# Linear attention and a gated convolution layer in one kernel: from four tokens a partition with 64-token tails to nine tokens a partition

## The chip, the cores and the metric

The kernel runs as one program on one core of a Trainium2 chip. Its engines are TensorE (PE: matmuls, with weight loads shown apart as PEld), VectorE (DVE), ScalarE (ACT), GpSimd (POOL) and SyncE (SP, which here only issues transfers). The metric is the device time of one execution in microseconds, smaller is better. Three executions of the kernel before gave 233.52, 234.02 and 235.5 us: the median is 234.02 us.

## The reference

Eight batches, eight heads, 576 tokens of 64 channels. First a linear attention, then a layer that multiplies a causal five-tap gate with a projection:

```python
def phi(x):
    proj = np.einsum('bhsd,df->bhsf', x, w_phi)              # 64 -> 128 features
    proj = proj - np.max(np.abs(proj), axis=-1, keepdims=True)
    return np.concatenate([np.exp(proj), np.exp(-proj)], axis=-1)
q_p, k_p = (phi(q), phi(k))
kv = np.einsum('bhsf,bhsd->bhfd', k_p, v)
z = np.sum(k_p, axis=2)
num = np.einsum('bhsf,bhfd->bhsd', q_p, kv)
den = np.einsum('bhsf,bhf->bhs', q_p, z)[..., None] + 1e-06
x = num / den                                                # then (8, 576, 8*64)
...
for k in range(K):                                           # K = 5 taps, causal
    gate_pre += conv_w[k][None, None, :] * xp[:, k:k + S, :]
gate = 1.0 / (1.0 + np.exp(-gate_pre))
val = x @ w_val                                              # 512 x 512
return (gate * val @ w_out).astype(np.float32)
```

Inputs and output are fp32; the matmuls take bf16 operands.

## The kernel before

**Tiling.** A batch's 576 tokens are split into a main part of 512 and a tail of 64. In the main part partition p holds the tokens 4p to 4p+3 of a head (four "planes" of 128 tokens). A unit is one pair of heads of one batch: 2 heads x 4 planes x 128 rows, 1024 tokens of two heads, in 32 main units; four tail units hold the tails of two batches and all eight heads each, again 1024 rows. So there are 36 units with the same work.

**Steps of a unit.** The names are those of the functions `op_...`; the lines are those of the profile.
- T (L331): eight 128x128 transposes of k and q into one PSUM bank; Tc (L224 on DVE, L222 on ACT) copies the 1024 columns to SBUF.
- PK and PQA (`tokproj`, L342): k and q times w_phi with tokens on the partitions, eight matmuls each, 64 rows deep, alternating between the two halves of the rows and between two PSUM banks. mKa, mK, mQa, mQ (L356) take the largest magnitude of each row, one bank (512 columns) at a time.
- K0 to K3 (L388): ACT takes exp of plus and minus the projected k, a bank each. The row maximum of k is not put in there: E (L382) makes exp of minus and plus the maximum, and V (L408, POOL) multiplies v by it and adds the column that gives z.
- PQ (L466): q's projection with features on the partitions; SH (L476): eight matmuls that subtract q's row maximum; Qa and Q (L484): four exps of a bank each.
- KV (L445, L450): per unit four sums (two signs, two heads) of four planes and a tail, 20 matmuls of full 128 rows with 65 columns; the tail rows of the other batch are kept at zero in VZ. KVM (L224, L222) copies them out.
- NUM (L509, tails L523): 16 matmuls of 65 columns; XN (L534, L536) divides by the last column; XP (L545, L548) brings channels back to the partitions by a DMA transpose from SP's queue into XT (main) or XH (tails).

**The layer.** GA (L604) makes the gate by matmuls with diagonal weights, 64x64 tiles, 32 matmuls for half of a batch's channels in two PSUM banks, with the shifts of planes split into up to two pieces a tap. TH (L612) is ACT's tanh over two banks, VAa and VAb (L617) the projection by w_val, GV (L633) gate times value on DVE, OUT (L642) the projection by w_out, OE (L649 on ACT, L651 on DVE) the halving on the way out of PSUM, ST (L663) the store. GAt, THt, GVt, OUTt, OEt, STt (L673, L681, L690, L695, L704, L716) do the same for the tails of two batches.

**Order.** All of it is one list written out by hand, `ORDER`: each word is a step, with its PSUM banks after @ and its engine after a colon. Every engine takes its instructions strictly in that order and waits for the operands and the banks that a step needs. The loads (L299, L304) are issued by POOL and turn fp32 to bf16 on the way; POOL's queue thus holds loads and the V steps in one order.

Of the kernel before, what the change touches and what calls it, by code (L numbers as in the profile page):

```python
# [20 lines left out]
SM = 512  # L21
ST = S - SM
E1 = D + 1
PL = 144
TL = 80
NG = B // 2
NU = 9 * NG

# [4 lines left out]
LD7 LD6 CK0 CQ0 T1@1 LD2 ND0:A W20 Tc1:D PK1@2,5 mKa1 PQA1@6,1 K01 mK1 mQa1 mQ1 T0@0 LD0 Tc0:A  # L33
PQ1@3,4 PK0@7,6 K11 K21 mKa0 T2@0 E1 Tc2:D K31 K00 SH1 Qa1 LD1 PK2@1,0 mK0 mKa2 LD3 mK2 PQA2@3,5
mQa2 ZV0:P LD8 K20 mQ2 T3@2 E0 Tc3:D PQA0@3,5 mQa0 mQ0 K02 K10 K30 E2 K22 PK3@7,6 mKa3 PQA3@2,5
LD4 mQa3 Q1 LD9 PQ2@3,4 SH2 LD10 mK3 K32 K12 T4@0 Tc4:D PK4@1,0 K03 Qa2 mQ3 V0:P K23 V1:P KV1@3 Q2
LD5 V2:P mKa4 K33 K04 KVM1:D NUM1@4 PQ3@6,3 SH3 mK4 XN1 LD11 K13 KV2@2 K24 LD31 PQA4@7,4 KVM2:D E3
mQa4 K14 mQ4 PQ0@1,5 K34 SH0 LD30 Qa3 Qa0 NUM2@6 PQ4@2,0 T5@4 T6@1 Q3 SH4 Q0 XN2 Qa4 E4 Tc5:D
Tc6:D PK5@7,6 mKa5 K05 PQA5@3,1 PK6@2,5 mQa5 Q4 LD13 K15 mK5 LD12 V3:P K25 KV3@3 mQ5 V4:P mKa6 K06
LC0 K35 KVM3:D E5 V5:P LD32 LD39 PQ5@0,1 TP0@7 mK6 Vb0:P NUM3@3 CW0 XP1 XN3 K16 XP2 T7@7 Tc7:D K26  # L40
SH5 Qa5 PQA6@6,2 mQa6 PK7@3,7 mKa7 KV4@4 PQA7@6,0 mQ6 mQa7 XP3 K36 T8@5 Tc8:D mK7 PQ6@2,6 Q5
KVM4:A SH6 K07 NUM4@4 mQ7 XN4 E6 PK8@0,1 K17 mKa8 Qa6 K27 T9@2 Tc9:D Q6 XP4 PQA8@3,5 V6:P PQ7@4,6
SH7 mQa8 LD15 mK8 K08 K37 PQA9@2,3 mQ8 mQa9 KV5@7 KVM5:D mQ9 T10@5 Tc10:D K18 PQ8@0,2 SH8 Qa7
PK9@4,7 mKa9 T11@3 E7 V7:P Q7 PK10@5,6 Tc11:D K28 mKa10 LD14 DG0:P Qa8 K38 KV6@3 Q8 K09 NUM5@0 mK9
KVM6:D NUM6@2 XN5 K010 mK10 KV7@0 K29 K110 XN6 K19 KVM7:D T12@5 PK11@1,4 mKa11 K210 HL0:P Tc12:D
XP6 LD16 K39 GA0@2 K310 mK11 K011 NUM7@6 VAa1@0 LD40 XN7 E8 VAb1 TH0 GV1 V8:P PK12@2,5 PQA10@3,6
K111 PQ9@1,7 SH9 VAa2@0 K211 mQa10 mKa12 LD19 VAa0@3 mK12 E9 LD17 K311 Qa9 VAb0 mQ10 KV8@4 KVM8:D
VAb2 GV0 PQA11@1,6 K012 V9:P Q9 mQa11 K212 PQ10@4,7 SH10 mQ11 K112 T13@3 Tc13:D NUM8@1 XN8 E10
K312 Qa10 Q10 GA1@5 TH1 PK13@3,4 mKa13 NUM0@1 V10:P KV10@7 XN0 KVM10:D XP5 XP0 XP8 E11 E12 K013
mK13 VAa3@5 GV2 PQ11@6,1 SH11 K113 Qa11 V11:P VAb3 GV3 LD18 K213 NUM10@2 XN10 T14@0 Tc14:D Q11  # L50
KV11@7 XP7 PQA12@5,6 K313 GA2@2 E13 TH2 PK14@0,1 mQa12 mQ12 PQA14@4,5 OUT1@6 OE1:A KVM11:D
PQA13@7,2 mQa14 V12:P V13:P mKa14 LD34 K014 mQ14 mQa13 K114 PQ12@3,4 SH12 XP10 KV12@6 mQ13 T15@5
Qa12 KVM12:A Tc15:D OUT2@7 Q12 mK14 K214 NUM11@2 E14 PQ13@0,6 SH13 Qa13 XN11 XP11 NUM12@4 OE2:D
XN12 T16@2 VAa6@3 PK15@7,0 mKa15 GA3@4 mK15 K314 V14:P VAa4@1 Q13 Tc16:D VAb4 K015 TH3 PQA15@6,2
GV4 K215 K315 PQ14@5,4 SH14 mQa15 K115 mQ15 VAa5@1 VAb5 PK16@0,6 Qa14 VAb6 Q14 KV13@7 GV5 mKa16
mK16 Vb9:P K016 VAa7@2 T17@1 GV6 E15 V15:P Tc17:D LD33 KVM13:A KV14@5 LD22 HL1:P NUM13@3 K116 K216
PQ15@0,7 KVM14:A VAb7 XN13 K316 SH15 GV7 PK17@1,3 mKa17 Qa15 K017 Q15 K117 LD35 mK17 XP13
# [42 lines left out]
OUT30@1 OEt3:A ST27 ST25 ST29 OE31:A ST28 STt3 ST31 OE30:D ST30  # L100
"""


class _U:
    pass

@with_exitstack
def kernel(  # L110
    ctx: ExitStack,
    tc: tile.TileContext,
# [30 lines left out]


    units = []
    for G in range(NG):
        for kind in range(9):
            u = _U()
            u.G = G
# [614 lines left out]
```

## Time and profile before

| what | before |
|---|---|
| three executions | 233.52, 234.02, 235.5 us |
| span of the profiled execution, first to last instruction | 232.5 us |
| mean granted TensorE clock in it | 0.972 |
| busy PE / DVE / ACT / POOL | 205.8 / 184.2 / 188.6 / 125.4 us |
| instructions PE / DVE / ACT / POOL | 3497 / 335 / 419 / 142 |
| DMA packets, bytes | 62002, 30.90 MB |
| queue of POOL's converting loads: packets, share of 16 engines | 36144, 58.2% |

The profile gives no time of its own for the profiled execution; its span of 232.5 us lies 1.5 us below the median of the three times, which hold the start and the end around the span as well. A busy time counts a matmul or a vector instruction from its start to its end, and neighbours on one engine overlap at their ends, so what an instruction costs its queue is the distance from its start to the next one's start, a little less than its duration.

### The profile page before, as it was taken

The numbers are of one execution on the slowest core, as the hardware profiler recorded it, in microseconds if no ns is written. First come the engines' busy times: TensorE is split into PE (matmuls) and PEld (weight loads), VectorE is DVE, ScalarE is ACT, GpSimd is POOL, SyncE is SP. The second block draws the span as 40 slices with busy tenths as digits, with TensorE's granted clock in tenths as the row PEclk, the third lists the DMA queues.
The fourth block names the chain that finished last, engine by engine and source line by source line (L and its number), as shares of the span: only waits on it lengthen the run. The fifth ranks groups of instructions, "written<-read, shape, count | busy, mean of one in ns | idle before, by whom it ended". The sixth has DMA issues, their size and how long they took to land.

```text
span 232.5 us, 8372 instructions
## 1 busy us (share of the span) xinstructions
PE 205.8 (89%) x3497; PEld 139.5 (60%) x3516; DVE 184.2 (79%) x335; ACT 188.6 (81%) x419; POOL 125.4 (54%) x142
## 2 busy tenths in 40 slices
PE   1286797888999989899999999999899999999991
PEld 1264675666666746567666766766476667564550
DVE  5559669999989979699999879897799788554451
ACT  3189869999997988599999979998899999934251
POOL 8909935999979437774919751564526241100000
PEclk9998579999999999999999999999999999999997
DMA  8997995979999942999994992499903928126195
GB/s 151 246 198 97 106 180 80 92 101 178 129 194 128 139 32 32 129 257 177 128 114 68 180 186 92 39 115 126 214 6 37 169 77 259 38 52 200 27 355 185
DMA packets 62002, 30.90 MB, mean 133 GB/s; under 512 B 33420, under 2 KB 59148, under 8 KB 61964
## 3 DMA queue, kind: packets, MB, share of 16 engines
q0 software_dynamic: 36144, 14.29, 58.2%
q1 hardware_dynamic: 25468, 15.78, 33.6%
q8 instruction: 27, 0.44, 0.8%
q10 hardware_dynamic: 352, 0.30, 0.4%
q14 instruction: 11, 0.09, 0.2%
HBM read 30.48 MB, written 9.44 MB: 172 GB/s over the span
## 4 chain that ended last, share of the span: by engine, by line
PE 69%; ACT 11%; DMA 9%; DVE 5%; issue 3%; SPq 1%; POOL 1%; POOLq 0%; DVEq 0%; ACTq 0%
PE PS L617 11%; PE PS L642 10%; PE PS L342 7%; PE PS L604 7%; PE PS L476 7%; PE PS L445 6%; PE PS L331 6%; DMA XT<-XN 6%; PE PS L509 5%; ACT QTIL L484 5%; ACT KTIL L388 3%; DMA kT<-in_k_dram 3%; PE PS L466 3%; PE PS L681 2%; DVE MQ L356 2%
## 5 line engine op out<-in xcount | busy, mean ns | idle before, releaser
L408 POOL TENSOR_TENSOR VT<-vN,E 128x1024 bf16<-128x1024 bf16 x27 | 51.5, 1907 | 60.4 <-issue 34.2
L388 ACT ACTIVATE KTIL<-PS 128x512 bf16<-128x512 f32 x128 | 76.7, 666 | 5.3 <-DVE MK L356 5.1
L484 ACT ACTIVATE QTIL<-PS 128x512 bf16<-128x512 f32 x128 | 71.0, 666 | 2.5 <-PE PS L476 1.1
L356 DVE TENSOR_REDUCE MK<-PS 128x4 f32<-128x512 f32 x72 | 47.9, 683 | 7.5 <-PE PS L342 7.2
L356 DVE TENSOR_REDUCE MQ<-PS 128x4 bf16<-128x512 f32 x72 | 47.4, 683 | 1.3 <-PE PS L342 1.2
L342 PE MATMUL PS<-W,T 64*128 64x128 bf16 x576 | 29.6, 227 | 5.8 <-DVE T L224 1.9
L617 PE MATMUL PS<-XT,WVAL 128*128 128x512 bf16 x128 | 33.8, 380 | 0.3 <-DMA XT<-XN 0.3
L342 PEld LDWEIGHTS <-T 64*128 64x128 bf16 x576 | 18.3, 98 | 21.8 <-issue 11.9
L642 PE MATMUL PS<-WOUT,GV 128*128 128x512 bf16 x111 | 29.9, 380 | 1.2 <-issue 0.5
L633 DVE SCALAR_TENSOR_TENSOR GV<-GATE,PS 128x512 bf16<-128x512 bf16 x32 | 21.6, 681 | 5.9 <-ACT GATE L612 3.1
L445 PE MATMUL PS<-VT,KTIL 128*128 128x65 bf16 x512 | 25.4, 198 | 0.8 <-DVE T L224 0.6
L536 DVE TENSOR_TENSOR XN<-PS,RCP 128x512 bf16<-128x512 f32 x36 | 24.9, 691 | 1.2
L445 PEld LDWEIGHTS <-KTIL 128*128 128x128 bf16 x512 | 22.8, 100 | 3.7 <-DVE T L224 0.8
L476 PE MATMUL PS<-nident,MQ 128*128 128x128 bf16 x288 | 23.9, 229 | 0.5 <-issue 0.5
L612 ACT ACTIVATE GATE<-PS 128x1024 bf16<-128x1024 f32 x16 | 16.7, 1044 | 8.8 <-PE PS L604 8.7
L476 PEld LDWEIGHTS <-MQ 128*128 128x128 bf16 x288 | 17.6, 102 | 9.5 <-issue 8.8
L224 DVE COPY T<-PS 128x1024 bf16<-128x1024 bf16 x31 | 21.1, 684 | 2.7 <-PE PS L331 2.3
L509 PEld LDWEIGHTS <-QTIL 128*128 128x128 bf16 x512 | 19.3, 99 | 5.5 <-DVE KVS L224 1.1
L509 PE MATMUL PS<-KVS,QTIL 128*128 128x65 bf16 x512 | 21.4, 196 | 1.3 <-DVE KVS L224 0.8
L450 PE MATMUL PS<-VZ,KTt 128*128 128x65 bf16 x128 | 21.9, 196 | 0.0
L604 PE MATMUL PS<-XT,DIAG 64*64 64x384 bf16 (+3 forms) x512 | 20.6, 299 | 1.0 <-issue 0.8
L642 PEld LDWEIGHTS <-GV 128*128 128x128 bf16 x128 | 11.3, 98 | 12.4 <-issue 0.6
(73 smaller groups left out, 304.1 us busy)
## 6 DMA issues: line engine op xcount, KB each, us to landing
out_dram<-OS SPq DMA_DIRECT2D x14, 512.0 KB, 3.8
kN<-in_k_dram POOLq DMA_DIRECT2D x7, 512.0 KB, 9.0
qN<-in_q_dram POOLq DMA_DIRECT2D x7, 512.0 KB, 8.4
vN<-in_v_dram POOLq DMA_DIRECT2D x7, 512.0 KB, 6.9
vF<-in_v_dram SPq DMA_DIRECT2D x2, 512.0 KB, 7.6
out_dram<-OSt SPq DMA_DIRECT2D x8, 128.0 KB, 2.4
out_dram<-OS SPq DMA_DIRECT2D x4, 256.0 KB, 2.9
qT<-in_q_dram POOLq DMA_DIRECT2D x8, 64.0 KB, 5.2
```

What stands on the lines that cost most here:

```text
L342: nc.tensor.matmul(PS[:, bank[rg], blk * P:(blk + 1) * P], u.T[r, i, blk, :], W2[r, :], start=True, stop=True,)
L356: nc.vector.tensor_reduce(dst, PS[:, bank, :].rearrange("p (b f) -> p b f", f=F), AX.X, ALU.max, apply_absolute_value=True,)
L388: nc.scalar.activation(u.KT[:, ft, rg, :, :].rearrange("p b f -> p (b f)"), PS[:, u.PK[rg], :], AF.Exp, scale=1.0 if ft == 0 else -1.0,)
L408: eng.tensor_tensor(dst[:, :, :, 0:D], x.unsqueeze(1).to_broadcast([n, 2, 8, D]), e.unsqueeze(3).to_broadcast([n, 2, 8, D]), ALU.mult,)
L445: nc.tensor.matmul(o, u.KT[:, ft, rg, h2 * 2 + j2, :], u.VT[:, ft, (h2 * 2 + j2) * 2 + rg, :], start=(c == 0), stop=False,)
L476: nc.tensor.matmul(PS[:, u.PQ[rg], blk * P:(blk + 1) * P], u.MQ[:, rg, blk:blk + 1].to_broadcast([P, P]), nident[:, :], start=False, stop= ...
L484: nc.scalar.activation(u.QT[:, ft, rg, :, :].rearrange("p b t -> p (b t)"), PS[:, u.PQ[rg], :], AF.Exp, scale=1.0 if ft == 0 else -1.0,)
L509: nc.tensor.matmul(ps[:, j2, x * E1:(x + 1) * E1], u.QT[:, ft, rg, h2 * 2 + j2, :], u.KVS[:, (ft * 2 + h2) * E1:(ft * 2 + h2 + 1) * E1], s ...
L536: nc.vector.tensor_tensor(u.XN[:, :, :, :], nv[:, :, :, 0:D], RCP[:, :, :].unsqueeze(3).to_broadcast([P, 2, 4, D]), ALU.mult,)
L604: nc.tensor.matmul(ps[c, par, j0 * P:j1 * P], DIAG[r, dt, 4 - dl, :], mv, start=(i == 0), stop=(i == len(parts) - 1), skip_group_check=True,)
L617: nc.tensor.matmul(PS[:, m.val[jt], :], WVAL[:, dt, jt * P:(jt + 1) * P], XTs[m.b % 2][:, dt, :, 16:PL], start=(dt == 0), stop=(dt == 3),)
L642: nc.tensor.matmul(PS[:, bank[0], :], m.GV[:, jt, j * P:(j + 1) * P], WOUT[:, jt, :], start=(jt == 0), stop=(jt == 3),)
```

## The change

The tokens are laid out anew: partition p of a half holds the nine tokens 9p to 9p+8 of a head, and the two heads of a pair lie in the two halves of the partitions (64 rows each). A main unit is a pair of heads and eight of the nine planes (2 x 8 x 64 = 1024 rows), 32 of them as before; the ninth planes of all heads of a batch make a tail unit of 512 rows, eight of them. One load brings a whole batch of k, q or v, tails included, in pieces of nine tokens; w_val and w_out come as fp32 from SP's queue and are converted by POOL.

- T: sixteen transposes of 64 rows into two banks; C copies them out in one instruction with its halves interleaved. KV: 36 matmuls of 64 rows, the two heads in two banks, no zero rows any more.
- MK, MQ, K0, K1, X0, X1: one instruction over two banks where there were two over one each.
- The gate: GF makes all four channel blocks of a batch in four banks, five taps of sixteen 32x32 tiles, 80 matmuls of 512 columns. A copy HL of the last four planes in front of the first ones, one row lower, gives the shifts whole, so no tap is split. GT, VT, HT, GW do the ninth plane of each batch; OT, OF, SU that of two batches.
- OUT is split into OA and OB of two matmuls each, as VA and VB are. Tail results, and the last batch's main ones, come back to XT by transposes on PE and a copy (XP with a bank, XX) instead of DMA transposes. Small tiles (row maxima, E, reciprocals, KV sums) get a place for every unit instead of rotating buffers, and `read` tells the scheduler that readers of a bank need not wait for readers of its earlier contents on other engines.
- A new `ORDER` with 1076 words for 1116.

Taps no longer go by 32 matmuls for half a batch but by 80 for a whole one; the steps that keep their count are OUT, VA/VB, NUM of the main units, SH of the main units. The core of the diff:

```diff
-        return src[name][b, h0:h1, 0:SM, :].rearrange("h (p j) d -> p h (j d)", j=4)
-
+        return src[name][b, 2 * h0:2 * h1, :, :].rearrange("(hp t) (p j) d -> (t p) hp (j d)", t=2, j=J)
...
+    def read(inst, bank):
+        for x in bank:
+            for other in gone[x]:
+                if other.engine != inst.ins.engine:
+                    tc.declare_no_dep(inst.ins, other, reason="covered by the wait for the matmuls")
+            held[x].append(inst.ins)
...
-                nc.tensor.transpose(u.Tps[:, n, blk, :], col(u, name, blk), ident_bf[:, :])
+                for h2 in range(2):
+                    r = slice(h2 * 64, h2 * 64 + 64)
+                    nc.tensor.transpose(
+                        u.Tps[:, h2, (4 * x + blk) * 64:(4 * x + blk + 1) * 64],
+                        main[name, u.b][r, u.hp, 2 * blk:2 * blk + 2, :].rearrange("p j d -> p (j d)"),
+                        ident_bf[r, r],
+                    )
...
+        copy(
+            eng, u.T[:, :, :, :].rearrange("p i b (h t) -> p h (i b) t", h=2),
+            u.Tps.rearrange("p h (x t) -> p h x t", t=64), u.TB,
+        )
...
-        nc.vector.tensor_reduce(
-            dst, PS[:, bank, :].rearrange("p (b f) -> p b f", f=F),
+        read(nc.vector.tensor_reduce(
+            dst[:, :, 0:n], banks(*bank)[:, :, c0:c0 + n * F].rearrange("p a (b f) -> p a b f", f=F),
...
+    def exps(dst, bank, n, ft):
+        read(nc.scalar.activation(
+            dst, banks(*bank)[:, :, 0:n * P].rearrange("p r (x t) -> p r x t", t=dst.shape[-1]),
...
     def op_KV(i, bank):
         u = units[i]
-        u.KVps = PS[:, bank[0], 0:4 * E1]
-        ut = tail_of[u.G]
+        t = units[32 + u.b]
+        u.KV = bank
         for ft in range(2):
-            for h2 in range(2):
-                o = u.KVps[:, (ft * 2 + h2) * E1:(ft * 2 + h2 + 1) * E1]
-                for c in range(4):
-                    j2, rg = c // 2, c % 2
+            for j in range(J):
+                for h2 in range(2):
+                    r = slice(h2 * 64, h2 * 64 + 64)
+                    if j < 8:
+                        kt, vt = u.KT[r, ft, j % 2, j // 2, :], u.VT[r, ft, j, :]
+                    else:
+                        kt, vt = t.KT[r, ft, u.hp % 2, u.hp // 2, :], t.VT[r, ft, u.hp, :]
                     nc.tensor.matmul(
-                        o, u.KT[:, ft, rg, h2 * 2 + j2, :],
-                        u.VT[:, ft, (h2 * 2 + j2) * 2 + rg, :],
-                        start=(c == 0), stop=False,
+                        PS[:, bank[h2], ft * E1:(ft + 1) * E1], kt, vt, start=(j == 0), stop=(j == 8),
                     )
-                nc.tensor.matmul(
-                    o, ut.KT[:, ft, h2, u.hp, :],
-                    VZ[u.G % 2][u.b % 2][:, ft, 2 * u.hp + h2, :],
-                    start=False, stop=True,
-                )
-
...
+            u.XPps = PS[:, bank[0], 0:128].bitcast(BF16).rearrange("p (a t) -> p a t", a=4)
+            for hp in range(HP):
+                for h2 in range(2):
+                    r = slice(h2 * 64, h2 * 64 + 64)
+                    nc.tensor.transpose(u.XPps[r, hp, :], u.XN[r, hp, :], ident_bf[r, r])
+            return
...
+        t = xt(b)[:, :, :].rearrange("p a (s c) -> p a s c", c=64)
+        copy(eng, t[:, :, 0:4, 1:64], t[:, :, 9:13, 0:63])
...
+    def taps(m, dts):
+        XT = xt(m.b)
+        for tap in range(5):
+            for dt in dts:
+                for r in range(4):
+                    rows, cols = slice(r * 32, r * 32 + 32), slice((r ^ dt) * 32, (r ^ dt) * 32 + 32)
+                    nc.tensor.matmul(
+                        PS[cols, m.gate[dt], :], DIAG[rows, dt, tap, :],
+                        planes(XT, rows, dt, tap),
+                        start=(tap == 0), stop=(tap == 4), skip_group_check=True,
+                    )
...
+    def op_GF(b, bank):
+        m = batches[b]
+        bank = sorted(bank)
+        for x in range(4):
+            m.gate[x] = bank[x]
+        taps(m, range(4))
...
+    def op_GT(b, bank):
+        m = batches[b]
+        m.tb = bank = sorted(bank)
+        XT = xt(b)
+        for s in range(2):
             for tap in range(5):
-                for dt, r, c, par in quarters(q2):
-                    nc.tensor.matmul(
-                        ps[c, par, q2 * P:(q2 + 1) * P], DIAG[r, dt, tap, :],
-                        XH[r, dt, :, 12 + tap:12 + tap + ST],
-                        start=(tap == 0), stop=(tap == 4), skip_group_check=True,
-                    )
+                for r in range(2):
+                    for x in range(2):
+                        dt = 2 * x + s
+                        rows = slice(r * 64, r * 64 + 64)
+                        cols = slice((r ^ x) * 64, (r ^ x) * 64 + 64)
+                        nc.tensor.matmul(
+                            PS[cols, bank[x], s * 64:s * 64 + 64], DIAG2[rows, dt, tap, :],
+                            XT[rows, dt, (8 + tap) * 64:(9 + tap) * 64],
+                            start=(tap == 0), stop=(tap == 4), skip_group_check=True,
+                        )
...
+    def op_OA(n, bank):
...
+        outmm(m.out[j], lambda jt: m.GV[:, jt, j, :, :].rearrange("p i t -> p (i t)"), (0, 1))
...
+    def outmm(bank, lhs, jts):
+        for jt in jts:
+            nc.tensor.matmul(PS[:, bank, :], lhs(jt), WOUT[:, jt, :], start=(jt == 0), stop=(jt == 3))
...
```

## The prediction

> **What bounds the kernel now.** I read the busy times first, then the busy times by stretch, then the chain that ended last, then single groups in the timeline to get prices. In the page:
>
> ```profile
> PE 205.8 (89%) x3497; PEld 139.5 (60%) x3516; DVE 184.2 (79%) x335; ACT 188.6 (81%) x419; POOL 125.4 (54%) x142
> ...
> PE 69%; ACT 11%; DMA 9%; DVE 5%; issue 3%; SPq 1%; POOL 1%; POOLq 0%; DVEq 0%; ACTq 0%
> ```
>
> Three engines are within 22 us of one another, and 69% of the chain is PE. The table by stretch (length, then busy us of PE, PEld, DVE, ACT, POOL, granted clock, DMA share, GB/s) shows how the bound moves:
>
> ```profile
> 30.00:60.00 30.00, 26.47 (x491) 19.56 (x488) 28.62 (x54) 28.53 (x68) 22.82 (x27) 0.97 1.10 124
> ...
> 180.00:210.00 30.00, 29.79 (x538) 20.04 (x544) 21.57 (x40) 24.20 (x54) 6.19 (x6) 1.00 0.56 126
> ```
>
> Up to 60 us DVE and ACT are full; later PE is. The chain in order of time (start, length, what) dates the change of bound and gives the first prices:
>
> ```profile
> 3.83 7.29 DMA kT<-in_k_dram
> ...
> 56.08 1.22 PE PS L604 x32
> ...
> 118.61 0.63 PE PS L523 x32
> ```
>
> The first taps run at 56.1 us, and from there to the last matmul's end at 227.7 nearly all pieces are PE. At the start 7.3 us go to the first tail load. After the last matmul come 4.8 us: a halving on DVE and the last store.
>
> **Prices.** Of a group that follows another without a gap I take start to start. In PE's timeline (start, length with the last one's drain, what):
>
> ```profile
> 142.03 0.40 PE L342 MATMUL PS<-W,T 64*128 64x128 bf16 x8
> 142.27 0.38 PE L466 MATMUL PS<-T,W 64*128 64x512 bf16 x2
> ...
> 144.26 0.39 PE L331 MATMUL PS<-ident_bf,kT 128*128 128x128 bf16 x4
> ...
> 144.70 0.29 PE L445 MATMUL PS<-VT,KTIL 128*128 128x65 bf16 x4
> ...
> 146.75 0.40 PE L342 MATMUL PS<-W,T 64*128 64x128 bf16 x8
> 147.08 1.04 PE L642 MATMUL PS<-WOUT,GV 128*128 128x512 bf16 x3
> ...
> 148.38 0.77 PE L673 MATMUL PS<-XH,DIAG 64*64 64x128 bf16 x40
> 149.08 1.07 PE L681 MATMUL PS<-XH,WVAL 128*128 128x128 bf16 x16
> 149.99 0.29 PE L445 MATMUL PS<-VT,KTIL 128*128 128x65 bf16 x4
> ...
> 150.62 0.66 PE L509 MATMUL PS<-KVS,QTIL 128*128 128x65 bf16 x16
> 151.11 0.29 PE L445 MATMUL PS<-VT,KTIL 128*128 128x65 bf16 x4
> ...
> 152.39 0.62 PE L476 MATMUL PS<-nident,MQ 128*128 128x128 bf16 x8
> 152.84 0.65 PE L509 MATMUL PS<-KVS,QTIL 128*128 128x65 bf16 x16
> ```
>
> - Projection of eight (L342): 0.24 us, if the next group has the same tile shape; 0.33 if PE changes the shape of its tiles (146.75 to 147.08). So a change of shape costs 0.1.
> - Transposes T: 0.44. SH: 0.45. KV: 20 matmuls 0.63, 31.5 ns each. NUM: 16 in 0.49. Tail taps L673: 40 in 0.70, 0.60 without the change, so 15 ns each although every one has its own weights. Tail value projection: 0.91.
> - Taps of half a batch (L604): 1.22 in the chain, 1.12 without the change. Tail NUM (L523): 32 in 0.63, 0.53 without it, 16.6 ns each. Four matmuls of 512 columns (L617, L642): 0.86. PQ, two of them side by side: 0.22, a quarter of that, though 0.33 pass to the next start.
> - ACT (start, length, what):
>
> ```profile
> 101.01 1.06 ACT L612 ACTIVATE GATE<-PS 128x1024 bf16<-128x1024 f32 x1
> 101.91 0.34 ACT L382 ACTIVATE E<-MK 128x8 f32<-128x8 f32 x2
> ```
>
> so two banks in one instruction take 0.90, where one bank takes 0.485 (pairs of L484 last 1.08 with an end of 0.11). On DVE 512 columns take 0.60 (L356 at 110.17, 110.77, 111.36), 0.53 of which are columns; 1024 in one instruction I take as 1.13, an estimate from these.
>
> **The change, PE.** Sum before: T 36 x 0.44 = 15.8; projections 72 x 0.24 = 17.3; PQ 7.9; SH 16.2; KV 32 x 0.63 = 20.2; NUM 15.7 and tails 2.1; taps 16 x 1.12 = 17.9; values and OUT 64 x 0.86 = 55.0; tail layer 4 x (0.60 + 0.91 + 0.86) = 9.5; together 177.6. In the order of before the tile shape changes 164 times: 16.4. Sum 194.0. From the first taps on it is 165.7, in 171.6 us that passed: PE is 96.5% packed.
>
> After, the new operations have no row of their own. T is 16 matmuls of 64 rows and 64 columns, alternating between the halves of the rows and two banks; KV 36 of 65 columns in the same form. Upper bound: the 29 to 31.5 ns of L342 and of KV now, that is 0.48 and 1.08 us. Lower bound: half a 65-column matmul (31.5 / 2 ns), about the 15 ns of L673. The nearest rows are L673 and L523, small tiles that take turns, at 15 and 16.6 ns; I take 15 to 15.5: T 0.24, KV 0.56. Taps: 80 matmuls with sixteen tiles at once; L604 streams four at once, 32 in 1.12. If sixteen do, 5 x 0.22 = 1.1 us a batch; at 15 ns each 1.2, which I take; if they overlap no better than four, 80 x 35 ns = 2.8.
>
> Sum after: T 32 x 0.24 + tails 8 x 0.23 = 9.5; projections 17.3; PQ 7.9; SH 16.2; KV 32 x 0.56 = 17.9; NUM 15.7 + 8 x 0.27 = 17.9; taps 8 x 1.2 = 9.6; GT 8 x 0.6 = 4.8 (40 matmuls a batch, not for two); VT 8 x 0.48 = 3.8; values, OUT, OT 58.4; transposes for XP 8 x 0.12 + 4 x 0.22 = 1.8; together 165.1. Tile shapes change 226 times in the new order: 22.6. Sum 187.7, 6.3 less than before: taps -8.3, T -6.3, KV -2.3; changes of shape +6.2, tail steps +4.
>
> The Trainium skill (TensorEngine Tiling, Restrictions and Gotchas) says that different row tiles cannot access one PSUM bank at a time; the taps of GF write four row tiles to each bank. In this trace L604 has two row tiles to a bank, and 32 x 512 columns in 1.12 us is four at a time, so the trace does not bear it out; by that rule the 2.8 of above would hold, 240 us, which is counted in (a).
>
> **ACT and DVE.** ACT before: 288 exps x 0.485 + 40 us of the rest = 180. After: 128 x 0.90 + 32 tail exps x 0.49 + the rest = 173. DVE before: row maxima 144 x 0.60 = 86.4, all 177. After: 64 x 1.13 + 16 x 0.60 = 81.9, two more copies (HL of 1008 columns about 0.8, between the 0.60 of T's copy and 1.2; XX), smaller tail steps: 181. So the two-bank steps save 7 us on ACT and DVE gains 4, hidden as long as PE is fuller: a batch has 23.1 to 24.2 us of PE and 22.2 to 22.7 of DVE. That cover is only 1 us a batch. POOL stays at about 123 (V 69 and 9, loads 30 x 0.95, conversion of the two weights about 9, diagonals 5); its V steps are late by nothing in this sum. The waits that `read` and the fixed small tiles take away I put at nothing: in the view of waits PE's largest sum for a vector engine after the start is 4.0 us (L342's weights for T's copy), so at most that would come back. The converting queue has fewer and longer pieces; on the chain its loads count only at the start.
>
> **The path.** Start: in before ACT's steps ahead of the first taps are 41.4 us by these prices, and the taps start at 56.1, so 14.7 us are lost to loads and first dependencies. After, the first GF stands behind only six K pairs, five Q pairs and two tails: ACT 27.0, DVE 26.9, PE 17.0, POOL 32.7. The same loss: 27.0 + 14.7 = 41.7 us, and POOL's 32.7 fit. From there PE has 187.7 - 17.0 = 170.7; packed like before, / 0.965 = 176.9, to 218.6. At the end of before four batches' layers were left to fill PE; now only the last batch's remain, behind XN, a transpose, XX and HL (0.85 + 0.2 + 0.35 + 0.8), about 3 us with little to run: 221.6. Then a halving 0.6 and a store of 128 KB, 2.4 by its row, 0.3 for the issue: 224.9. With the 1.5 us by which before's median exceeds its span, 226.4: I say 227, 3% below 234.02. Its own range is 220 to 233: the start 4 us either way, packing 0.95 to 0.98, KV and T 3 us more.
>
> **Rivals.**
> (a) Small matmuls have a floor: at 29 ns KV is 1.04 and T 0.46, 32 x 0.70 = 22 us more, at 22 ns half of it: 238 to 250. Taps that overlap only four at once (2.8) would add 8 x 1.6 = 13: 240. For it: full-array KV and NUM go at 31 ns now; against it: L673 and L523 at 15 to 17 ns with weights of their own. It turns the result slower from about 19 ns on. The Trainium skill (TensorE: Matmul & The Clock Gate, Wait — 56ns, not 53.3ns?) gives 25 ns as the least distance; by it this rival would hold, near 250, but L673 goes below it here.
> (b) DVE becomes the bound: C now writes with its halves interleaved. If that copy costs a cycle per column like the fp32 steps, 1.13 instead of 0.60, DVE has 4 x 0.53 = 2.1 more a batch, 24.5, and passes PE's 23.7; in the 30 us from 90 on, with every engine in play, DVE was 0.91 busy, and 24.5 / 0.91 is 26.9 us a batch where the forecast has 24.6 (23.7 / 0.965); over seven batches 16: 243, slower. It decides from about 0.83 us a copy. Against it: T's copy takes 0.60 for 1024 now, and its inner runs stay 64 long.
> (c) Banks: GF takes four of eight banks at once, until two tanhs of 0.90 have read them, and T, PK, PA, PQ, KV, N take two each. If PE stands 1.7 us a batch for want of banks, 8 x 1.7 = 14: 240, slower; it decides from 0.9 us. Nothing in before shows it, its gate took two.
> (d) More gain: fewer loads and maxima bring the first GF to 36 us, PE packed 0.98: 36 + 174.2 + 3 + 3.3 + 1.5 = 218.
>
> **How the numbers follow.** The forecast 0.48, (a) 0.15, (b) 0.13, (c) 0.10, (d) 0.14. A measurement of this kernel tells apart about 1%. Faster by more: nearly all of the forecast (0.45), all of (d), and some 0.05 of mild forms of (a) to (c): 0.64. Within 1%: 0.08. Slower: 0.28. The range takes (d) and the middle of (a) to (c): 217 to 242.
>
> **What would show it.** Right: GF in about 1.3 us with 80 matmuls; KV's 36 in 0.56 and T's 16 in 0.24; first GF near 42 us; two-bank exps 0.90 apart, row maxima 1.13; PE between 180 and 200 busy and the chain mostly PE. Wrong: KV near 1 us (a); DVE the first in the chain with copies over 0.83 (b); PE waiting before GF, T or PK for ACT or DVE readers of its banks (c).

## The result and the profile after

The changed kernel took 256.54 us (median of 253.63, 259.45, 257.75 and 255.33), the kernel before in the same runs 234.12. The ratio is 1.086, with a 95% interval of 1.080 to 1.092: 8.6% slower, where 3% faster was forecast. Ratios here and below leave out executions in which the whole core ran disturbed, and each stands against the kernel before on the same chip; medians take in all. The profiled execution is the one of 253.63 us, with a span of 251.8. Its page:

```profile
PE 206.3 (82%) x4730; PEld 134.3 (53%) x4756; DVE 186.8 (74%) x295; ACT 184.1 (73%) x305; POOL 110.2 (44%) x142
...
PE 55%; DVE 15%; DMA 13%; ACT 10%; issue 5%; SPq 1%; ACTq 0%; DVEq 0%
```

PE is busy as long as before (205.8) in a span that is 19 us longer, and PE's part of the chain fell from 69% to 55%. What grew there are DVE, DMA and "issue". The table by stretch (columns as before) tells where:

```profile
30.00:60.00 30.00, 25.04 (x635) 16.90 (x634) 24.39 (x39) 24.42 (x40) 21.57 (x31) 0.94 0.73 102
60.00:90.00 30.00, 21.98 (x531) 13.94 (x529) 19.32 (x32) 19.18 (x31) 10.13 (x12) 0.83 0.79 116
90.00:120.00 30.00, 25.63 (x539) 15.61 (x541) 20.69 (x32) 21.32 (x37) 10.31 (x11) 0.83 0.81 140
...
180.00:210.00 30.00, 26.59 (x642) 17.01 (x646) 25.40 (x39) 24.82 (x46) 11.27 (x13) 1.00 0.27 60
```

Before 60, PE, DVE and ACT are each some 25 of 30 us busy. From 60 to 90 none is above 22, and the granted clock falls to 0.83 in two stretches. The chain in order of time (start, length, what) names what stands there:

```profile
35.45 5.06 DMA XT<-XN
41.73 2.36 PE PS L585 x80
...
65.03 11.24 DMA XT<-XN
78.04 2.29 PE PS L585 x80
...
97.87 8.35 DMA XT<-XN
107.16 1.86 PE PS L585 x39
110.71 1.08 PE PS L585 x30
137.30 1.34 PE PS L585 x80
```

L585 is the taps GF. The first one starts at 41.73; the next ones start 36.2, 29.2, 30.1, 25.9, 27.8, 27.8 and 18.2 us after one another. Ahead of three of them stands a DMA transpose of XN into XT.

The prices themselves are as forecast. PE's timeline (start, length, what), then DVE's:

```profile
152.95 0.43 PE L441 MATMUL PS<-VT,KT 64*128 64x65 bf16 x16
153.22 0.19 PE L441 MATMUL PS<-VTt,KTt 64*128 64x65 bf16 x2
153.25 0.42 PE L441 MATMUL PS<-VT,KT 64*128 64x65 bf16 x16
153.51 0.19 PE L441 MATMUL PS<-VTt,KTt 64*128 64x65 bf16 x2
153.54 0.39 PE L355 MATMUL PS<-W,T 64*128 64x128 bf16 x8
...
154.85 0.29 PE L333 MATMUL PS<-ident_bf,kN 64*128 64x64 bf16 x8
154.97 0.28 PE L333 MATMUL PS<-ident_bf,qN 64*128 64x64 bf16 x8
```

```profile
126.84 1.21 DVE L373 TENSOR_REDUCE MKA<-PS 128x8 f32<-128x1024 f32 x1
127.97 1.21 DVE L373 TENSOR_REDUCE MQA<-PS 128x8 bf16<-128x1024 f32 x1
...
76.69 0.68 DVE L198 COPY T<-PS 128x1024 bf16<-128x1024 bf16 x1
77.29 0.42 DVE L198 CAST KVSA<-PS 128x260 bf16<-128x260 f32 x1
```

KV's 36 matmuls take 153.54 - 152.95 = 0.59 us, eight transposes 0.12, a maximum over two banks 1.13, the copy with interleaved halves 0.60. The two-bank exps are 1.02 to 1.03 long on average (64 of k, 64 of q); two that follow one another take 1.93 to 1.95, so 0.91 to 0.92 from start to start.

**The stall.** POOL, DVE and PE around 65 us (a bracket gives the idle time before an instruction and what ended it):

```profile
57.50 0.81 POOL L312 DMA_DIRECT2D kN<-in_k_dram  x1
58.30 0.75 POOL L312 DMA_DIRECT2D qN<-in_q_dram  x1
59.04 0.76 POOL L312 DMA_DIRECT2D vN<-in_v_dram  x1
59.77 0.77 POOL L312 DMA_DIRECT2D kN<-in_k_dram  x1
```

```profile
76.35 0.43 DVE L198 COPY XT<-XT 128x1008 bf16<-128x1008 bf16 x1 [6.28 <-DMA XT<-XN]
...
77.43 0.61 PE L355 MATMUL PS<-W,T 64*128 64x128 bf16 x8 [6.29 <-DVE T L198]
```

Four loads of 576 KB each go out in one bunch. The four transposes of batch 1, issued from 59.7 to 65.0, land 11.2 to 13.4 us after their issue. The copy HL.1 waits for the last of them at the head of DVE's queue, and C, which PE's next projections need, waits behind it: DVE and PE stand for 6.3 us.

Late transposes are not new. Here the 28 of XN into XT land after 2.4 to 13.4 us with a median of 4.1. In the kernel before (the 32 transposes; then PE's waits for them from the first taps on: sum, number, longest):

```profile
DMA to landing us min/median/max: 2.5/4.6/10.4
...
PE PS L617 <- DMA XT<-XN: 0.3, 1, 0.3
PE PS L604 <- DMA XT<-XN: 0.2, 1, 0.2
```

They landed hardly sooner there, but PE waited only 0.5 us for them.

**The gaps.** A second loss shows as idle time of PE that nothing released, in the middle of a step:

```profile
110.71 1.08 PE L585 MATMUL PS<-XT,DIAG 32*32 32x512 bf16 x31 [1.69 <-issue]
...
166.23 1.14 PE L585 MATMUL PS<-XT,DIAG 32*32 32x512 bf16 x64 [2.42 <-issue]
...
194.02 0.43 PE L585 MATMUL PS<-XT,DIAG 32*32 32x512 bf16 x15 [1.73 <-issue]
```

With two more (1.62 at 104.79, 0.66 at 146.87) they make 8.1 us. Ahead of the five stand 1752, 1880, 2644, 3024 and 3660 matmuls: the distances between them are multiples of 128 or within 4 of one (some records are missing in a trace). 128 matmuls with their weight loads are 256 instructions of PE.

### The profile page after: what moved, and what is told of

Its sections match the earlier page's. It is cut to its first block, busy times and chain, and to the rows that moved or that the text cites. A ratio compares the mean times of both kernels' runs of the same rounds, so it can differ in the third digit from the quotient of the medians.

```text
span 251.8 us, 10562 instructions
## 1 busy us (share of the span) xinstructions
PE 206.3 (82%) x4730; PEld 134.3 (53%) x4756; DVE 186.8 (74%) x295; ACT 184.1 (73%) x305; POOL 110.2 (44%) x142
## 4 chain that ended last, share of the span: by engine, by line
PE 55%; DVE 15%; DMA 13%; ACT 10%; issue 5%; SPq 1%; ACTq 0%; DVEq 0%
PE PS L614 11%; DMA XT<-XN 10%; PE PS L643 8%; PE PS L585 6%; PE PS L464 6%; PE PS L506 5%; PE PS L441 5%; PE PS L355 4%; DVE MQA L373 4%; ACT QT L398 3%; PE PS L455 3%; DMA cw<-in_moe_conv_w_dram 3%; DVE MKA L373 3%; DVE XN L526 2%; ACT KT L398 2%
## 5 line engine op out<-in xcount | busy, mean ns | idle before, releaser
L423 POOL TENSOR_TENSOR VT<-vN,EA 128x1024 bf16<-128x1024 bf16 x32 | 60.9, 1903 | 105.0 <-issue 68.4
L398 ACT ACTIVATE KT<-PS 128x1024 bf16<-128x1024 f32 x64 | 62.8, 1028 | 15.6 <-PE PS L355 15.2
L398 ACT ACTIVATE QT<-PS 128x1024 bf16<-128x1024 f32 x64 | 62.5, 1024 | 6.3 <-PE PS L464 5.5
L373 DVE TENSOR_REDUCE MKA<-PS 128x8 f32<-128x1024 f32 (+1 forms) x40 | 44.3, 1111 | 5.7 <-ACT KT L398 4.8
L373 DVE TENSOR_REDUCE MQA<-PS 128x8 bf16<-128x1024 f32 (+1 forms) x40 | 44.4, 1111 | 4.1 <-PE PS L355 3.9
L355 PE MATMUL PS<-W,T 64*128 64x128 bf16 x512 | 25.5, 229 | 10.2 <-DVE T L198 7.9
L643 PE MATMUL PS<-WOUT,GV 128*128 128x512 bf16 x105 | 30.1, 380 | 1.2 <-issue 0.6
L441 PE MATMUL PS<-VT,KT 64*128 64x65 bf16 x1024 | 24.2, 195 | 1.9 <-issue 0.9
L441 PEld LDWEIGHTS <-KT 64*128 64x128 bf16 x1024 | 20.5, 97 | 7.9 <-issue 3.1
L464 PE MATMUL PS<-nident,MQA 128*128 128x128 bf16 x288 | 24.0, 226 | 0.0
L506 PE MATMUL PS<-KVSA,QT 128*128 128x65 bf16 x512 | 22.1, 196 | 2.0 <-ACT KVSA L196 1.1
L526 DVE TENSOR_TENSOR XN<-PS,RCPA 128x512 bf16<-128x512 f32 x32 | 22.1, 691 | 1.6 <-DMA XT<-XN 0.6
L585 PE MATMUL PS<-XT,DIAG 32*32 32x512 bf16 x640 | 15.1, 469 | 8.9 <-issue 5.8
L614 PEld LDWEIGHTS <-WVAL 128*128 128x128 bf16 x128 | 10.8, 103 | 13.8 <-issue 6.7
L333 PE MATMUL PS<-ident_bf,kN 64*128 64x64 bf16 x256 | 10.2, 197 | 7.4 <-DVE kN L198 5.4
```

The lines of the kernel that those rows point to most:

```text
L355: nc.tensor.matmul(PS[:, bank[par], c0 + blk * P:c0 + (blk + 1) * P], u.T[r, i, blk, :], W2[r, :], start=True, stop=True,)
L373: read(nc.vector.tensor_reduce(dst[:, :, 0:n], banks(*bank)[:, :, c0:c0 + n * F].rearrange("p a (b f) -> p a b f", f=F), AX.X, ALU.max, ap ...
L398: read(nc.scalar.activation(dst, banks(*bank)[:, :, 0:n * P].rearrange("p r (x t) -> p r x t", t=dst.shape[-1]), AF.Exp, scale=1.0 if ft = ...
L423: e.tensor_tensor(u.VT[:, :, :, 0:D], x.unsqueeze(1).to_broadcast([P, 2, n, D]), w.unsqueeze(3).to_broadcast([P, 2, n, D]), ALU.mult,)
L441: nc.tensor.matmul(PS[:, bank[h2], ft * E1:(ft + 1) * E1], kt, vt, start=(j == 0), stop=(j == 8),)
L464: nc.tensor.matmul(PS[:, u.PQ[par], blk * P:(blk + 1) * P], MQA[:, i, par, blk:blk + 1].to_broadcast([P, P]), nident[:, :], start=False, s ...
```

## Theories

A: the loads reach the time by way of the transposes, which they hold up on the DMA engines just where the order leaves no room for it. Narrow form: only because HL blocks DVE's queue. B: PE is short of instructions when short matmuls use up a block faster than the next one comes. C: the engines are coupled more tightly in the new order, so that any wait costs. D (formed late): the instruction blocks come through the DMA engines, and are late when these are full.

## Experiments

**1. The loads left out, after and before.** `if b > 2: return` ahead of the loads, and k, q and v of batch b % 3 read in their place; in the kernel before the loads and tails alike.

> Leaves out the loads of k, q and v of batches 3 to 7; these batches compute on what batches 0 to 2 brought. Theory A (loads in bursts): four converting loads issued within 3 us hold the DMA engines, the transposes of XN behind them land after 8 to 13 us instead of 4, the halo copy HL waits for them at the head of DVE's queue, PE stands 6 us and then runs at half clock. Then here the transposes land in 2.5 to 5 us, PE's long waits ahead of the second and third GF are gone, and the time falls from 253.6 to 230 to 238 us. Theory B (PE runs out of instructions, the gaps of 1.6 to 2.4 us inside a step that name no releaser, 8 us in all): such gaps stay, if the loads have nothing to do with them, and the time falls by less than 10 us. Theory C (two-bank steps and a gate over four banks make the engines wait for one another all the time): within 5 us of 253.6.

> The kernel before the change, without the loads of k, q and v of batches 3 to 7 and of the tails of the last four batches; it computes these on the data of earlier ones. If loads cost every order of this kind as much as they cost the new one (17 us), it falls from 233.5 to about 217. Theory A: in the old order 25 to 87 steps lie between a batch's last transpose and its first taps, so it hides them: 229 to 233.5 us, under 4 us gained.

Changed kernel: 237.32 us, ratio 1.016 [1.006, 1.026]. Kernel before: 230.52, ratio 0.984 [0.980, 0.988]. The loads cost the new order 1.086 - 1.016 = 7% of 234, 16 us, and the old one 4. Transposes now land after 2.4 to 7.9 us (median 2.6), and from 60 to 90 PE is full again, at full clock:

```profile
60.00:90.00 30.00, 28.42 (x744) 19.30 (x742) 27.62 (x45) 27.84 (x49) 12.82 (x14) 1.00 0.23 46
```

So most of the loss is the loads', though the loads carry the same bytes as before. The two profiles (251.8 and 235.0 us of span) say where they cost. The wait of 6.3 us ahead of GF.1 is gone. The gaps of PE that nothing released fall from 9.2 to 3.0 us, all small ones from the first GF on included. And the stretches with a granted clock of 0.50, from just ahead of the first GF to the last matmul, shrink from 23.8 us (41.4 to 44.8, 72.2 to 82.4, 106.3 to 116.5) to 6.8; by comparing each matmul in them with its like at full clock I estimate 7.7 and 3.1 us of PE's time for them. About 7 us to the old order without loads remain.

**2. The loads moved.** First those of batch n+2 right behind HL.n:

```diff
-V.7:P LD.15 LD.16 ... T.9@4,5 LD.17 LD.18
+HL.1:D LD.15 LD.16 LD.17
```

> Only the places of the loads in POOL's order are changed: the three loads of batch n+2 stand right behind the halo copy of batch n (n = 1 to 5), when no transpose is under way, instead of in bursts ahead of the transposes. Theory A: the transposes of batch 1 land in about 4 us, PE's wait of 6.3 us before the second GF and the one before the third go, the clock stays up: 236 to 244 us. Theories B and C: the loads are the same in number, so 250 to 256.

252.86 us, ratio 1.073 [1.058, 1.088], which overlaps the interval of the change. All transposes land within 7.5 us, but the loads are now too late for the tails' transposes (L319) of their own batch:

```profile
PE PS L319 <- DMA qN<-in_q_dram: 7.9, 5, 2.8
...
PE PS L319 <- DMA kN<-in_k_dram: 3.0, 1, 3.0
```

The columns are the sum, the number and the longest of the waits. One wait took the other's place. Then the loads right behind the last transpose of a batch, a batch earlier:

```diff
+LD.14 LD.15 LD.16 ... XP.7 LD.17 LD.18 LD.19 LD.20 ... XP.11 LD.21 LD.22 LD.23
```

> Only places of loads in POOL's order change. When the loads stood right behind the halo copy for the batch after next they came too late (PE waited 8.7 us in all for q of the next tail). Here k and q of batch 3 follow those of batch 2, and each later batch is loaded a whole batch earlier, right behind the last transpose of batch 1, 2, 3, 4. Theory A (it is the meeting of loads and transposes on the DMA engines that costs): transposes land in 2.5 to 5 us, no step waits for a load, the kernel comes near the one without loads of batches 3 to 7 (237.3): 238 to 244 us. If loads cost by their mere number of bytes, wherever they stand: 248 to 256.

250.55 us, 1.067 [1.057, 1.078]. POOL ran ahead and issued loads into the transposes of the batch after (longest 13.3 us, GF.4 waits 5.4 us). Neither place is free of both.

**3. HL on POOL** (`HL.0:D` to `HL.0:P`, batches 0 to 3 and 5; 4 and 6 had it there already), so that the wait for the transposes blocks nothing on DVE.

> The halo copy HL of batches 0 to 6 is put on POOL, whose queue has room, instead of six on DVE. Theory A in its narrow form (what costs is that DVE's queue stands behind HL): copies and maxima go on while HL waits, PE has work until GF itself needs the halo, gain 4 to 8 us: 246 to 250. If the late transposes alone count, GF still waits as long and the gain is under 3 us. Theories B and C: no change, or 2 us longer by POOL's slower copy, 1.03 us for 0.43.

258.18 us, 1.106 [1.093, 1.120]. The wait stands in front of GF instead:

```profile
PE PS L580 <- POOL XT L193: 10.1, 4, 6.7
PE PS L580 <- issue: 6.5, 3, 2.6
```

The narrow form of A falls. The late transposes cost, not the queue in which they are waited for.

**4. Transposes earlier or by PE.** Each XP right behind its XN instead of in a bunch:

```diff
-... OE.0:D XP.6 XP.5 XP.4
+XN.4 XP.4 ... XN.5 XP.5 ... XN.6 XP.6
```

> In the order of the change the DMA transposes of a batch's first three units wait to be issued until the third is done, in one bunch just ahead of the next gate. Here each stands right behind its XN. Nothing else moves. Theory A (transposes behind loads hold the gate): units 4 and 5 are transposed before the four loads of 57.5 to 60.5 us are issued, only the last one or two of a batch can be late; the waits ahead of the second and third GF shrink from 6.3 us to 2 to 4: 246 to 251 us. Theory B (PE short of instructions) and C (engines bound together): 253 to 257, no difference.

259.37 us, 1.103 [1.095, 1.111]. In batch 0 only two of the transposes now stood ahead of the load of w_out on SP's queue; the other two were issued behind it, from 40.98 on, and GF.0 came at 52.2 after a wait of 11.8 us. So this run can't show what the later batches gained. The same with the last main unit of batches 0 to 6 by PE and a copy (XP with a bank, XX on ACT):

> As the kernel with early transposes, and the last main unit of batches 0 to 6 is transposed by PE and copied by ACT, as the tails are, so that no DMA stands between a batch's last XN and its HL except those issued 10 us and more before. Theory A: the long waits ahead of GF go, 238 to 247 us, PE 7 x 0.3 us more. Theory C: PE waits in its own queue for XN of the last unit, some 1 us a batch: 250 to 257. Theory B: gaps without a releaser stay at 5 to 8 us in all, in both.

248.29 us. A median of four executions that lie from 246.07 to 286.27, with no interval, so only its profile counts: 244.3 of span, with 4.4 us still lost ahead of GF.0 for the reason above. All transposes of batches 0 to 6 by PE, none by DMA:

> All transposes of XN for batches 0 to 6 go by PE (four matmuls of 128x128 into a free bank) and a copy on ACT or DVE by turns, no DMA transposes; the loads stand where they were, in bursts. Theory A: HL no longer waits for a DMA; PE gets 28 x 0.22 = 6 us of work and some 4 us of tile shape changes, ACT and DVE 14 copies each (7 and 5 us); the waits of 6.3 and 2.5 us and the half clock after them go: 240 to 247 us. If the loads hurt PE in another way (its gaps without a releaser), the gaps grow with 112 more matmuls and the time stays at 250 to 258.

261.2 us, 1.116 [1.108, 1.124]. No wait for a DMA transpose is left, but PE waits for DVE's and ACT's steps in many small portions, 25 us in all from the first GF on. That is C: PE's banks and the copies XX are not free. It speaks against taking everything off the DMA engines, not against A.

**5. The rest of the change.** The declarations in `read` taken out, and the two-bank maxima and exps as one instruction a bank:

> The declarations that a reader of a bank need not wait for other engines' readers of its earlier contents are left out (the fewer waits of the change undone). By the prediction they are worth 0 to 4 us; the waits for the matmuls cover them, so 253 to 257 us, no difference.

> Every exp and every row maximum over two banks is split into two over one bank (the two-bank steps undone). By the prices of the profile before ACT gets 144 x 0.07 = 10 us more and DVE 72 x 0.07 = 5. Theory C (two-bank steps bind the engines together): no loss or a gain, 248 to 256. If ACT and DVE are near the bound after all: 258 to 264. Theory A: about 256 to 260, since part of it falls into waits for the transposes.

258.26 us, 1.104 [1.095, 1.113], and 259.09 us, 1.108 [1.100, 1.116]. Both ratios lie some 2% above that of the change. So these parts gain 4 to 5 us each, if anything, and are not the loss.

**6. Taps as 40 matmuls of 64x64 tiles** instead of 80 of 32x32 (`DIAG2[rows, dt, tap, :]`, two row and two column tiles).

> The gate of a batch goes by 40 matmuls of 64x64 tiles with the diagonals that the ninth plane uses, instead of 80 of 32x32. Theory B: fewer instructions, the gaps without a releaser inside the gate (5.8 us) go; the gate itself takes 5 x 2 x 0.22 = 2.2 us instead of 1.25, 8 us more in all, so about 253 to 258. If the gaps are no matter of the instruction count they stay and the time is 258 to 262. Theory A: up to 8 us more where PE sets the end, less where the batch waits anyway: 256 to 261.

257.83 us (253.35 to 258.79), no verdict. In the profile the gaps shrank from 9.2 to 1.7 us, and the taps got some 7 us longer: no net change.

**7. Batch 0 as in the change; early transposes and the last unit by PE for batches 1 to 6.** Then the same with loads one at a time, and with the taps of 64x64.

```diff
-XN.33 N.8@4,5 ... XP.7
+XN.33 N.8@4,5 XP.7@0 ... XX.7:A
```

> The change with two steps altered in batches 1 to 6: each DMA transpose is issued as soon as its unit's XN is there instead of in one bunch with the last one, and the last main unit of a batch comes back to XT by transposes on PE and an ACT copy. Batch 0 stays as in the change. The loads are left where they are, in bursts of three and four. Theory A (the loads reach the time by way of the last transposes of a batch, which they hold up on the DMA engines): PE's waits for XT ahead of GF.1 to GF.6 fall below 2 us each, the first GF stays at 41.7, and of the 17 to 19 us that the loads cost 10 to 14 come back: 241 to 246 us. Rival C (PE, DVE and ACT are coupled so tightly in the new order that a wait taken away comes back as other waits): 250 to 256. The gaps of PE without a releaser (rival B, instruction supply) are not touched by it: 3 to 8 us of them stay, in steps that release nothing.

242.55 us, 1.034 [1.027, 1.040]: 12 us by the ratios, 14 by the medians, with all loads where they were, and the time is what A had forecast. The wait behind C fell from 7.9 us with a longest of 6.3 to

```profile
PE PS L350 <- DVE T L193: 2.9, 3, 2.1
```

But the 12 us are not the transposes' alone. The gaps that nothing released, which this edit was not meant to touch, fell from 9.2 to 4.3 us as well; PE's matmuls are other ones here, so the ends of its blocks (experiment 8) fall elsewhere. PE's work got some 4 us longer in return, a difference of the same estimate at full clock.

> As the kernel before it in this list (early transposes, the last unit of batches 1 to 6 by PE), with the loads of batches 3 to 5 one at a time, each behind a V step of its own, instead of in bursts of three and four. Theory A: the remaining cost of the loads is in their bursts; transposes land in under 6 us at most, and the time is 2 to 4 us below that kernel: 238 to 244. Rival: what remains are the gaps of PE without a releaser and the coupling, which the loads' places do not touch: within 1.5 us of that kernel, or slower where a load comes later than its first T (then PE waits for k or q by DMA).

247.52 us, 1.054 [1.046, 1.062]: slower, though transposes land no later (median 4.3, longest 9.3). What grew in the profile are the gaps of PE without a releaser, from 4.3 to 8.7 us; but this profile is of the longest of the four executions, 250.41 us, so that alone is weak evidence for a second way of the loads to the time.

> As the first kernel of this list, with the taps of GF as 40 matmuls of 64x64 tiles instead of 80 of 32x32 (the same sums). The taps themselves get 0.9 to 1 us longer a batch, 7 us in all. Rival B (PE runs dry of instructions in steps of many short matmuls): the gaps without a releaser fall from 3 to 8 us to under 2, so that the time changes by -1 to +4 us. If the gaps cost nothing on the path (they would be waits for the vector engines anyway), the full 7 us are added: 248 to 253.

252.23 us, 1.076 [1.068, 1.083]. Half as many taps, and the gaps stay (4.7 us for 4.3); the slower taps are paid in full. In experiment 6 the same step had taken the gaps from 9.2 to 1.7 us. So fewer instructions do not remove the gaps by themselves, and B falls in its simple form; that short taps have a part in them is not excluded.

**8. The instruction blocks.** The profile of the change has a queue for instructions. The kernel before has 27 packets in it, the change

```profile
q8 instruction: 37, 0.61, 1.0%
```

PE's matmuls and weight loads number 3497 + 3516 = 7013 before and 4730 + 4756 = 9486 after; divided by 256 that is 27.4 and 37.1. Each packet is one block of 256 PE instructions, 0.61 MB / 37 = 16 KB. The Trainium skill (Runtime: NRT & Kernel Launch, Instruction fetch mechanics) says this of the blocks, 256 instructions in 16 KB, and the count agrees. It also says that crossing a block's end is mostly hidden: most of the 37 cost nothing here either, but five cost 0.7 to 2.4 us. Shortly before the gap of 1.69 us, which starts at 109.02 (queue, packets, MB, share of the 16 DMA engines in the window from 108.0 to 108.5):

```profile
q1 hardware_dynamic: 62, 0.19, 96.3%
q8 instruction: 1, 0.02, 12.9%
```

q1 is SP's queue, which had issued six stores of 256 KB from 99.23 on; they fill the DMA engines when the block is due. At the two other long gaps the packet starts within 1 us of the gap too, and SP's queue had issued six and two stores of 256 KB just before. The records of the packets say what is late. All 37 take 0.88 to 1.56 us, those of the five gaps 0.92 to 1.14, and PE goes on 2.3 to 2.5 us after the start of its packet at each of the five. So the transfer is not slower at a gap; it starts late. Hence D, and three runs. The main stores of batches 0 to 4 left out of the change:

> The change with the stores of the main results of batches 0 to 4 left out (ten steps ST, twenty transfers of 256 KB); all the rest, the loads and the tail stores too, is as in the change. In the change's profile the instruction queue moves 37 packets of 16 KB, one for each 256 of PE's matmuls and weight loads, and in each of the three long gaps of PE that release nothing (1.69, 2.42 and 1.73 us, in GF.2, GF.4 and GF.5) the packet starts within 1 us of the gap's start while stores of 256 KB fill the DMA engines. Theory D (the instruction packets are late behind the stores): these three gaps fall below 0.6 us each, the sum of all gaps without a releaser from 8.1 to under 3, and the time by 5 to 9 us, to 247 to 252. Theory B (the packets are late only because 128 short matmuls are used up faster than a packet comes): gaps of over 1 us stay at the same counts of matmuls, and the time changes by less than 3 us.

247.44 us, 1.057 [1.051, 1.063]: 7 us less by the ratios. The sum of the gaps fell from 9.2 to 3.0 us. The gap in GF.2 is gone (a wait of 1.76 us for a copy by DVE stands ahead of GF.2 instead), those in GF.4 and GF.5 fell from 2.42 and 1.73 us to

```profile
161.56 1.14 PE L580 MATMUL PS<-XT,DIAG 32*32 32x512 bf16 x64 [1.63 <-issue]
...
187.90 0.44 PE L580 MATMUL PS<-XT,DIAG 32*32 32x512 bf16 x15 [0.53 <-issue]
```

The 1.63 is above the 0.6 that D had set. Between 155 and 161.5 a load and two tail stores remain there, with the queue of converting loads at 72.1% of the engines. The 0.53 in GF.5 cannot be D: from 183.6 to 187.4 the packet itself is all that the DMA engines move. That the short taps outrun the block there, which is B, fits it. The rest of the 7 us fits the clock, whose stretches at 0.50 fell from 23.8 to 10.2 us.

> The kernel with early transposes and the last unit of batches 1 to 6 by PE (242.55 us), with the main stores of batches 0 to 5 moved to right behind the GF of the next batch, where PE has the large value matmuls ahead of it, instead of 40 to 90 steps later shortly before the next GF. Theory D (instruction packets late behind the stores): the gaps that release nothing (4.5 us in its profile) fall below 2, 238 to 241 us. Theory B: the same within 1.5 us.

241.05 us, 1.031 [1.028, 1.035]: not told apart from the 1.034 of the kernel it stands on. The gap in GF.2 is gone, but one of 1.87 at 73.7, among the loads, is still there and smaller ones are new; their sum is 4.8 us, where D had set less than 2. To move the stores alone is not enough while the loads fill the engines.

> The kernel with early transposes and the last unit of batches 1 to 6 by PE (242.55 us), with the loads of batches 3 to 7 left out as in the kernel that did this to the change (237.32 us). Theory A (the loads reached the time by way of the last transposes alone): 240 to 243, nothing more is to be had from the loads. If they cost by a second way as well (by PE's instruction packets, or by late k and q): 234 to 238.

238.08 us, 1.021 [1.015, 1.026]: 3 us by the ratios, 4.5 by the medians, so the loads did cost by a second way. Which one, the same piece of the order shows, the projection just ahead of GF.1, first with loads (two stretches with the columns of the table by stretch, then the timeline), then without:

```profile
70.00:72.40 2.40, 2.09 (x88) 1.68 (x85) 2.31 (x6) 2.40 (x4) 0.59 (x2) 1.00 1.21 209
72.40:73.90 1.50, 0.02 (x2) 0.01 (x1) 0.50 (x1) 0.09 (x1) 0.00 (x0) 1.00 1.22 207
...
72.02 0.39 PE L350 MATMUL PS<-W,T 64*128 64x128 bf16 x7
73.89 0.23 PE L350 MATMUL PS<-W,T 64*128 64x128 bf16 x1 [1.48 <-issue]
74.05 1.35 PE L580 MATMUL PS<-XT,DIAG 32*32 32x512 bf16 x80
```

```profile
70.00:72.40 2.40, 2.19 (x93) 2.03 (x89) 2.28 (x6) 2.40 (x4) 1.16 (x2) 1.00 0.00 0
...
72.59 0.40 PE L353 MATMUL PS<-W,T 64*128 64x128 bf16 x8
72.92 1.47 PE L583 MATMUL PS<-XT,DIAG 32*32 32x512 bf16 x80
```

With full DMA engines (1.21) PE does seven of the eight matmuls and then stands 1.48 us for a block; with idle ones it does all eight and goes on. The packet of this block, the ninth in both, starts at 71.49 with loads, after 2448 recorded instructions of PE, and at 68.89 without, after 2264. The gaps from the first GF on sum to 1.5 us instead of 4.3. So D is shown at two places, for stores in GF.2 and for loads here. It is not all, as the 0.53 above shows. That a packet waits in the DMA engines' own queues fits its late start, but was not tried.

## Why the prediction was wrong

| step of the prediction | forecast | measured |
|---|---|---|
| first GF | 41.7 | 41.73 |
| KV, T, GF | 0.56, 0.24, 1.2 | 0.59, 0.24, 1.34 with its end of 0.1 |
| two-bank maximum; exp | 1.13; 0.90 | 1.13; 0.91 to 0.92 |
| DVE, ACT busy | 181, 173 (prices without ends) | 186.8, 184.1 |
| PE's work from the first GF to the last matmul | 170.7 | 181.2 busy |
| PE's waits from there to the last matmul | 6.2 + 3 | 23.0 |
| last matmul to the end | 3.3 | 5.9 |

- **Right:** the start and the prices, though two of its signs failed: PE is 206.3 us busy, not 180 to 200, and only 55% of the chain. The start owes part of that to luck: its 14.7 us of loss were carried over from before, with an own range of 4 us either way, and the chain here ends in a transpose of 5.06 us and a copy HL of 1.05, which the sum does not list. Rival (a) is out: KV's matmuls are 16.4 ns apart, 0.59 us / 36, far from the 22 to 29 ns it needs. By the Trainium skill (TensorE: Matmul & The Clock Gate, Wait — 56ns, not 53.3ns?) the least is 25 ns; the trace does not agree. Nor does it bear out that row tiles cannot share a bank (TensorEngine Tiling, Restrictions and Gotchas): the sixteen tiles of GF, four row tiles to a bank, each on a quarter of the partitions of its own, do 80 matmuls in 1.34 us. Rival (b) is out: the interleaved copy costs 0.60, not 0.83 or more. Rival (c) is out as the cause: the largest waits of PE come from transposes and instructions, not from readers of banks.
- **The step that failed first:** "on the chain its loads count only at the start". That was read from the chain of before. There each transpose of the main units stands 27 or more words of the order ahead of the half of the taps that reads it (17 in the last batch), and PE waited 0.5 us for them. After, the last transpose of a batch stands 16 to 36 words ahead of HL, and the other units' transposes are issued in a bunch shortly before it. Loads of the same bytes then decide: 16 us (experiment 1), 6.3 of them in the one wait ahead of GF.1, the rest in the gaps and the low clock. Experiment 7 gets 12 us back with the loads where they were, part of it by fewer gaps; another 3 come back with the loads left out (experiment 8). A cleaner split by way was not measured.
- **The step that failed next:** "packed like before, / 0.965". Beside the transposes it left out what 9486 instead of 7013 PE instructions need, one block of 16 KB for each 256. The gaps that release nothing were 2.2 us before and 9.2 after, from the first taps on.
- **A term that was put at nothing:** the clock. From the first taps on the granted clock was 1.00 in the kernel before, and the same sum (165.7) met PE's busy time there (166.2). After, it is 0.94: 0.50 in the 23.8 us named in experiment 1. The first two stretches begin in PE's waits ahead of GF.0 and GF.1, the third 1.5 us after the gap of 1.62. There GF takes 2.36 us instead of 1.34. By the estimate of experiment 1 this is 7.7 of the 10.5 us by which PE is busy longer than 170.7.
- **What is left of PE's work:** some 3 us. Without the loads 178.1 us are left, 3.1 of them by the clock. The large matmuls are not it: from start to start "values, OUT, OT 58.4" are 65.7 there, but 4.8 of these are 50 changes of tile shape at 0.095 us (0.311 from start to start ahead of a change, 0.216 else), which the forecast has in its 22.6, and 2.1 are the clock, which leaves 58.8. Where the 3 us lie was not found.
- **The end:** 5.9 instead of 3.3 us. The last matmul ends at 245.9, but ACT's last halving starts only at 247.20, behind store issues on its own queue (the last of 0.50 us at 246.66), and after it comes one more store.
- **Summed up:** span forecast 224.9, measured 251.8, 26.9 more: 13.8 of waits (23.0 - 9.2), 10.5 of PE's busy time, most of it clock, 2.6 at the end. The forecast had no rival that said "a transfer of the new order meets the loads"; the DMA engines' share had been looked at in the kernel before only.

No kernel here that does all the work beat the one before. The best with all loads and stores, which has early transposes, the last unit by PE and early stores, is 3.1% slower. With late transposes and the loads both out of the way the new order still takes 238.1 against 230.5 us of the old one without these loads; the cause of these 7.6 us stays open.

## What to carry to other kernels

When an order is rewritten, list for every transfer between two engines how far ahead of its reader it is issued and what else is on the DMA engines then; a DMA transpose that was hidden by distance is priced at its landing time under load, not at its time alone. Count PE's instructions as well as their time: shorter matmuls are free only as long as a block of 256 comes in time, and the blocks share the DMA engines with loads and stores. A long wait of PE costs more than its length when the clock is low after it. Prices of single operations can all be right and the sum wrong by 12%: forecast the waits of the new order, not the share of waiting in the old one.

## What the runs showed of the hardware that was not expected

- A DMA transpose that lands in 2.4 us on quiet DMA engines took 11.2 to 13.4 us behind four converting loads of 576 KB.
- PE's instructions come in packets of 16 KB, each for 256 matmuls and weight loads. In the change each takes 0.88 to 1.56 us, also where PE stands for it. With full DMA engines it starts late, and PE stood 0.5 to 2.7 us at the end of a block.
- The granted clock was 0.50 from 72.2, in PE's wait ahead of GF.1, to 82.4, and from 106.3 to 116.5; it was 1.00 from 137.3 to 147.0, where GF.3 comes without a wait. 80 taps took 2.36 us at the low clock and 1.34 at the full one.
